# Fused attention and two expert layers on one core: the second half block's softmax in block 0 made on both groups at once and later

## The chip, the cores and the metric

One core of one Trainium2 chip. The metric is the device time of one execution in microseconds (us). The engines are TensorE (PE), VectorE (DVE), ScalarE (ACT), GpSimd (POOL) and the queue of the DMA issues (SP). Before the change three runs took 837.55 us in the median.

## What is computed

The reference is an attention over compressed keys and values, a gated layer, and a layer of eight experts of which each token takes two:

```python
a = softmax over the sequence of phi                      # 4 x 8 heads, 576 positions, 32 memory rows
k_m = einsum('bhsm,bhsd->bhmd', a, k)                     # 32 compressed keys a head
v_m = einsum('bhsm,bhsd->bhmd', a, v)
scores = (q @ k_m.T) / 8                                  # 576 x 32 a head
attn = exp(scores - max) / (sum(exp(scores - max)) + 1e-9)
x = attn @ v_m                                            # 2304 tokens of 512
g = x @ w_gate;  x = (silu(g) * (x @ w_val)) @ w_out      # 1536 wide
# then noisy top-2 gating over 8 experts, each relu(x @ w1) @ w2, summed with the gate's weights
```

Products that need float32's accuracy are made of three passes over tensors that are split in a high and a low part.

## The kernel before

**Blocks and slots.** The 2304 tokens are worked in eight half batches of 288 tokens, called blocks 0 to 7 (`BT = 288`, `NB = 8`). A block has twelve slots, one for each 128 columns of the gated layer (`NF1 = 12`). In a slot PE makes the gate and value products `pg` and `pv` (`gv`, L473, six products of 288 columns each) and the output products of two slots before (`down`, L502 in block 0, L506 later). ACT takes the tanh of `pg` (L481), DVE multiplies (`gate_act`, L486 and L487: "gate f" below is this step of slot f). L486 is also the last reader of the bank that the next slot's `pg` is written to. Block 0 differs from the others: its slots also unpack the packed weights w_a, in two halves, `top` on ACT (L204) and `low` on DVE (L208), and every second slot makes a projection of v_m with the gate and value weights (`proj_a` on PE, L346, with name pp; `proj_h` on ACT, L438, and `proj_b` on DVE, L443, its high and low parts, name pt).

**The softmax of a block.** It has two groups g of 128 rows (head parity), each a tile of 128 x 9 x 32. `s2_p` makes the scores on PE (psc), `s2_t` transposes them to SBUF on DVE (sm, L364), `s2_a` takes maxima and subtracts them (DVE, L370, L371), `s2_e` the exponential (ACT, L375), `s2_b` is `s2_sum` (sum, + 1e-9, reciprocal: L379 to L381) and `s2_norm` (scaling L386, transposition back L391), `s2_c` copies the result as the high part of X on ACT (L401), and `s2_d` subtracts it to get the low part on DVE (L404). X[i] holds both parts of both groups. In `gv` of a block i > 0 the first product reads group 0's high part and the second reads its low part.

**What sets the order.** All is written out by hand. `put(i, n, fn)` notes a step for a place n of block i, and `run(i, n)` carries out what is noted up to n; place 2f is the start of slot f, 2f + 1.5 lies behind its `gv`, and 2f + 1.99 is its end. The table `AT` has the places; the loop at L746 reads the list "s2" of block i - 1 for the softmax of block i, ten places: scores, transposition, maxima, exponential, then three for each group (`s2_b`, `s2_c`, `s2_d`). A pair of numbers splits a step: for maxima and exponential into group 0 and group 1. Each engine works its own instructions strictly in the order in which the program issues them. In block 0 the list makes the second half block's softmax X[1]: scores in slot 6, transpositions at 14, maxima at 17 and 17.9, exponentials at 17.1 and 19, group 0's sums at 19, group 1's at 21.1, the last subtraction at 23. "(1, 0)" below is slot 0 of block 1, where X[1] is first read.

The lines of `slot0` that set the order inside a slot of block 0:

```python
    gv(0, f)
    run(0, 2 * f + 1.5)
    ...
    gate_act(0, f)
    for k in todo:
        step(k)
    run(0, 2 * f + 1.99)
```

Of the kernel before, what the change touches and what calls it, by code (L numbers as in the profile page):

```python
# [7 lines left out]
F32 = mybir.dt.float32  # L8
# [12 lines left out]
B, H, S, D, M = 4, 8, 576, 64, 32  # L21
# [5 lines left out]
BT = S // 2  # L27
# [20 lines left out]
        2: (9, 9.92, 13.2, 13.9, 15, 17.9, 19, 19.9, 21, 21.9, 23, 23.9, 25, 25.9, 27),  # L48
    },
# [20 lines left out]
def r(ap):  # L70
    return ap.bitcast(F32R)
# [3 lines left out]
def moe_program(ctx, tc, xin, wa, wgn, nz, wb, out):  # L75
# [35 lines left out]
    gpool = right.enter_context(tc.tile_pool(name="gate", bufs=1, side="right"))  # L111
    att = left.enter_context(tc.tile_pool(name="att", bufs=1))
# [108 lines left out]
    for n in range(len(HOMES)):  # L221
# [26 lines left out]
    e_cap = const.tile([128, E], F32, name="e_cap")  # L248
    G.iota(e_cap, pattern=[[T, E]], base=CAPS, channel_multiplier=0,
           allow_small_or_imprecise_dtypes=True)  # L250
    kz = [const.tile([128, 2, 1 + n, D], F32, name=f"kz{n}") for n in range(2)]
    G.memset(kz[1], 0.0)
    TOP = [w1pool.tile([128, 2 * DM], FP16, tag="OS", name="top", bufs=4) for _ in range(4)]
    for t in TOP:
        G.memset(t, 0.0)
# [57 lines left out]

    def s1_cv(b, g, s=2, eng=None):
        st = ST[b, g][1]
        out = kz[g][:, :, g, :] if s == 2 else kz[g][:, s, g, :]
        p = TP.pop((b, g, s))
        if eng is None:
            V.tensor_scalar(out, p, st[:, 2:3], None, op0=OP.mult)
        else:  # L320
            A.activation(out, p, AF.Copy, scale=st[:, 2:3])

    def s1_d(b, g, s=2):

# [23 lines left out]
    def s2_p(i):  # L348
        p = [other([128, BT], "psc") for n in range(2)]
        by_heads(p, KM[i // 2][:, 0], QT[i])  # L350
        SM[i] = p

    def s2_first(g):

        p = {g: other([128, BT], "psc")}
        by_heads(p, KM[0][:, 0], QT[0], (g,))
        SM[0, g] = att.tile([128, BT // M, M], F32, tag="sm", name="sm", bufs=2)
        V.transpose(SM[0, g].rearrange("p a m -> p (a m)"), p[g])

    def s2_t(i):  # L360
        p = SM.pop(i)
        for n in range(2):
            SM[i, n] = att.tile([128, BT // M, M], F32, tag="sm", name="sm", bufs=2)
            V.transpose(SM[i, n].rearrange("p a m -> p (a m)"), p[n])  # L364

    def s2_a(i, g):
        na = BT // M
        sm = SM[i, g]
        rd = att.tile([128, 3, na], F32, tag="rd", name="rd", bufs=2)
        V.tensor_reduce(rd[:, 0, :], sm, axis=AX.X, op=OP.max)  # L370
        V.tensor_sub(sm, sm, rd[:, 0, :, None].to_broadcast([128, na, M]))  # L371
        SM[i, g] = (sm, rd)

    def s2_e(i, g):
        A.activation(SM[i, g][0], SM[i, g][0], AF.Exp, scale=1.0 / D ** 0.5)  # L375

    def s2_sum(i, g):
        sm, rd = SM[i, g]
        V.tensor_reduce(rd[:, 1, :], sm, axis=AX.X, op=OP.add)  # L379
        V.tensor_scalar(rd[:, 1, :], rd[:, 1, :], 1e-9, None, op0=OP.add)  # L380
        V.reciprocal(rd[:, 2, :], rd[:, 1, :])  # L381

    def s2_norm(i, g):
        na = BT // M
        sm, rd = SM[i, g]
        V.tensor_mul(sm, sm, rd[:, 2, :, None].to_broadcast([128, na, M]))  # L386
        if i or not g:
            at = att.tile([128, BT], F32, tag="at", name="at")
        else:
            at = gpool.tile([128, 2, 2, BT], F32, tag="x", name="ex")[:, 0, 0, :]  # L390
        V.transpose(at, sm.rearrange("p a m -> p (a m)"))  # L391
        SM[i, g] = at

    def s2_b(i, g):
        s2_sum(i, g)
# [350 lines left out]
    for i in range(1, NB):  # L746
        if i > 1:
            put(i - 1, 6, load_q, i)
        n = AT["s2"].get(i - 1, AT["s2"][2])
        put(i - 1, n[0], s2_p, i)  # L750
        put(i - 1, n[1], s2_t, i)
        for g in range(2):
            for m, fn in zip((n[2], n[3], *n[4 + 3 * g:7 + 3 * g]), (s2_a, s2_e, s2_b, s2_c, s2_d)):
                if fn is s2_b and isinstance(m, tuple):
                    put(i - 1, m[0], s2_sum, i, g)
                    put(i - 1, m[1], s2_norm, i, g)
                else:
                    put(i - 1, m[g] if isinstance(m, tuple) else m, fn, i, g)
# [802 lines left out]
```

## Time and profile before

| | us |
|---|---|
| median of 3 runs (lowest, highest) | 837.55 (836.06, 838.38) |
| the profiled execution | 840.57 |
| its span, first to last instruction | 838.8 |
| busy: PE, DVE, ACT, POOL | 824.1, 636.9, 391.6, 244.5 |
| mean granted clock of PE | 0.999 |

The profiled execution's time is a little above its span: what lies around the first and the last instruction is in the time and not in the span. Times in the rows below are counted from the span's start. A busy time alone does not tell what an engine costs; the chain of waits, followed back from the last instruction, does.

### The profile page before, as it was taken

How to read it: one execution, taken by the hardware profiler on the slowest of the kernel's cores; microseconds unless marked ns; L12 is line 12 of the kernel's file. 1: busy time of each engine (PE TensorE's matmuls, PEld its weight loads, DVE VectorE, ACT ScalarE, POOL GpSimd, SP SyncE). 2: the span in 40 equal slices, each digit the busy share in tenths (PEclk: the TensorE clock that was granted, in tenths of full speed). 3: DMA queues.
4: the chain of work that ended last, by engine and by line, in shares of the span. 5: the costliest groups of instructions: out<-in, count | busy, mean ns of one | idle time of the engine just before them, and what ended most of it. 6: DMA issues, size and time to landing. Idle time of an engine off the chain costs nothing.

```text
span 838.8 us, 16650 instructions
## 1 busy us (share of the span) xinstructions
PE 824.1 (98%) x6320; PEld 732.4 (87%) x6320; DVE 636.9 (76%) x1535; ACT 391.6 (47%) x804; POOL 244.5 (29%) x345
## 2 busy tenths in 40 slices
PE   8999999999999999999999999999999999999996
PEld 6777989999999998999999878988888888888885
DVE  5887688766867587868784597898889988899771
ACT  5765565333433334343444555446445454554430
POOL 2000012424243242553122223322415234145232
PEclk9999999999999999999999999999999999999999
DMA  9993649865327363449756983645574654654521
GB/s 345 402 399 122 199 161 326 256 221 151 106 74 219 86 209 85 132 115 234 212 173 174 231 234 73 137 134 119 121 168 104 158 127 99 164 139 111 161 85 64
DMA packets 79145, 143.20 MB, mean 171 GB/s; under 512 B 16176, under 2 KB 36880, under 8 KB 79056
## 3 DMA queue, kind: packets, MB, share of 16 engines
q1 hardware_dynamic: 59696, 100.66, 38.9%
q0 software_dynamic: 19360, 41.38, 20.8%
q8 instruction: 52, 0.85, 0.4%
q14 instruction: 37, 0.30, 0.1%
HBM read 105.34 MB, written 36.68 MB: 169 GB/s over the span
## 4 chain that ended last, share of the span: by engine, by line
PE 80%; DMA 8%; DVE 6%; issue 3%; ACT 1%; SPq 1%; POOL 1%; POOLq 0%; DVEq 0%; ACTq 0%
PE acc L1194 18%; PE ph L1178 17%; PE acc L506 16%; PE pg L473 10%; PE pv L473 9%; PE pp L346 3%; DMA xs<-R,gidx 2%; PE acc L502 2%; DMA wb<-wb 2%; DMA out<-pv,ix 1%; PE pT L528 1%; DMA early<-wa 1%; PE ph L987 1%; DMA kv<-xin 1%; PE pkv L310 1%
## 5 line engine op out<-in xcount | busy, mean ns | idle before, releaser
L1194 PE MATMUL acc<-ws,hs 128*128 128x512 f32 (+1 forms) x690 | 175.0, 394 | 0.0
L1178 PEld LDWEIGHTS ph<-xh,ws 128*128 128x128 f32 x1008 | 151.0, 188 | 9.7 <-ACT y L1217 0.7
L1178 PE MATMUL ph<-xh,ws 128*128 128x308 f32 x1008 | 157.4, 304 | 0.3 <-ACT y L1217 0.3
L1194 PEld LDWEIGHTS acc<-ws,hs 128*128 128x128 f32 (+1 forms) x690 | 122.7, 184 | 24.4
L506 PE MATMUL acc<-a,ro 128*128 128x288 f32 x576 | 116.4, 295 | 0.0
L1032 POOL DMA_INDIRECT out<-pv,ix x40 | 62.9, 1572 | 175.8 <-ACT pv L1024 65.5
L506 PE MATMUL acc<-a,os 128*128 128x288 f32 x432 | 106.0, 295 | 0.0
L473 PE MATMUL pg<-x,pt 128*128 128x288 f32 x576 | 101.3, 310 | 0.7 <-DVE pt L443 0.2
L473 PEld LDWEIGHTS pg<-x,pt 128*128 128x128 f32 x576 | 80.9, 188 | 18.5 <-issue 6.8
L506 PEld LDWEIGHTS acc<-a,ro 128*128 128x128 f32 x576 | 92.1, 188 | 0.0
L473 PE MATMUL pv<-x,pt 128*128 128x288 f32 x576 | 91.9, 295 | 0.0
L473 PEld LDWEIGHTS pv<-x,pt 128*128 128x128 f32 x576 | 81.7, 188 | 0.0
L670 POOL DMA_INDIRECT xs<-R,gidx x48 | 47.9, 999 | 115.9 <-DMA xs<-R,gidx 99.4
L486 DVE SCALAR_TENSOR_TENSOR ta<-ta,pg 128x288 f32<-128x288 f32 x84 | 37.7, 449 | 54.1 <-ACT ta L481 54.0
L506 PEld LDWEIGHTS acc<-a,os 128*128 128x128 f32 x432 | 74.1, 188 | 0.3 <-ACT ro L459 0.2
L481 ACT ACTIVATE ta<-pg 128x288 f32<-128x288 f32 x84 | 34.4, 409 | 80.9 <-PE pg L473 79.9
L463 POOL DMA_DIRECT2D os<-osl x72 | 40.8, 567 | 98.0 <-PE acc L506 57.9
L492 ACT ACTIVATE a<-ta 128x288 fp32r<-128x288 f32 x84 | 37.3, 444 | 68.5 <-DVE ta L487 66.7
L987 PE MATMUL ph<-xt,wm 128*128 128x384 f32 (+1 forms) x256 | 55.3, 306 | 0.0
L987 PEld LDWEIGHTS ph<-xt,wm 128*128 128x128 f32 x256 | 43.7, 189 | 2.6
L487 DVE TENSOR_TENSOR ta<-ta,pv 128x288 f32<-128x288 f32 x84 | 38.2, 454 | 8.7
L493 DVE TENSOR_TENSOR a<-ta,a 128x288 fp32r<-128x288 f32 x84 | 37.6, 448 | 5.8 <-ACT a L492 5.6
(241 smaller groups left out, 1453.0 us busy)
## 6 DMA issues: line engine op xcount, KB each, us to landing
wb<-wb SPq DMA_DIRECT2D x70, 512.0 KB
os<-osl POOLq DMA_DIRECT2D x72, 256.0 KB
kv<-xin SPq DMA_DIRECT2D x16, 576.0 KB
xl<-xs SPq DMA_DIRECT2D x40, 160.0 KB
stg<-wa SPq DMA_DIRECT2D x12, 511.8 KB
out<-zt SPq DMA_DIRECT2D x1, 5888.0 KB
xd<-R SPq DMA_DIRECT2D x8, 603.0 KB
qt<-xin SPq DMA_DIRECT2D x8, 576.0 KB
```

The costliest lines, as they stand in the source:

```text
L463: G.dma_start(r(lo), r(osl[f][:, :]))
L473: P.matmul(p, r(PT[f // 2, g][:, w, f % 2, 128 * a:128 * a + 128]), r(X[i][:, s, g, :]), start=(n == 0), stop=(n == 5))
L486: V.scalar_tensor_tensor(ta, ta, 1.0, pg, op0=OP.add, op1=OP.mult)
L487: V.tensor_mul(ta, ta, pv)
L492: A.activation(r(ah[:, 0, :]), ta, AF.Copy)
L493: V.tensor_sub(r(ah[:, 1, :]), ta, ah[:, 0, :])
L506: P.matmul(ACC[i][c], r(OS[i, f][w][:, o]), r(ah[:, s, :]), start=(f == 0 and n == 0), stop=(f == NF1 - 1 and n == 2))
L670: G.indirect_dma_start(out=xs[:, :], out_offset=bass.IndirectOffsetOnAxis(ap=RT[i][:, t, n:n + 1], axis=0), in_=R[i][:, t, :], in_offset=None)
L987: P.matmul(p, r(w[:, c]), r(x[:, k, b, :]), start=(m == 0), stop=(m == 11))
L1032: G.indirect_dma_start(out=out, out_offset=bass.IndirectOffsetOnAxis(ap=IX[e][:h, t:t + 1], axis=0), in_=PV[e, t][:h], in_offset=None, com ...
L1178: P.matmul(out, r(w[i][:, c + 128 * k:c + 128 * k + 128]), r(x[:, m, k, a]), start=(start and n == 0), stop=(n == 5), skip_group_check=not ...
L1194: P.matmul(AC2[e, t][:h, cols], r(HS[p][a][:, n, o]), r(w[b][:, n, cols]), start=(f == 0 and m == 0), stop=(f == NF2 - 1 and m == 2), skip ...
```

## The change

For block 0's list "s2" there are now seven places in the place of ten, which the loop takes as "both groups in one": maxima and subtraction at 21 (behind `gv` of slot 10), exponential at 21.02, sums to transposition at 21.9 (end of slot 10), copy at 22 (start of slot 11), subtraction at 23.55 (end of slot 11). To make that possible both groups lie in one tile (sm, rd and at), and each step takes a group number or 2 for both. Other blocks keep their places and still go group by group, in the new tiles. Three small things come with it: the first block's subtractions are one instruction, group 1's own tile `ex` is gone, and the two tiles kz with a padding of zeros become one without.

```diff
     "s2": {
-        0: (13.9, 14, (17, 17.9), (17.1, 19), 19, 19.9, 21, 21.1, 21.9, 23),
+        0: (13.9, 14, 21, 21.02, 21.9, 22, 23.55),
...
-    kz = [const.tile([128, 2, 1 + n, D], F32, name=f"kz{n}") for n in range(2)]
-    G.memset(kz[1], 0.0)
+    kz = const.tile([128, 2, 2, D], F32, name="kz")
...
-                P.transpose(p[:64 * g + 64, m, :], kz[g][:, m].rearrange("p n d -> p (n d)"), ident)
+                P.transpose(p[:64 * g + 64, m, :], kz[:, m, :g + 1].rearrange("p n d -> p (n d)"), ident)
...
+    na = BT // M
+
+    def groups(g):
+        return slice(0, 2) if g == 2 else slice(g, g + 1)
+
+    def flat(t, g):
+        return t[:, groups(g)].rearrange("p g a m -> p (g a m)")
+
+    def sm_tile(i):
+        SM[i, "s"] = att.tile([128, 2, na, M], F32, tag="sm", name="sm", bufs=1)
+        SM[i, "r"] = att.tile([128, 3, 2, na], F32, tag="rd", name="rd", bufs=1)
...
+    def s2_parts(i, g):
+        sm, rd = SM[i, "s"], SM[i, "r"]
+        sm = sm[:, groups(g)].rearrange("p g a m -> p (g a) m")
+        return sm, [rd[:, k, groups(g)].rearrange("p g a -> p (g a)") for k in range(3)]
+
     def s2_a(i, g):
-        na = BT // M
-        sm = SM[i, g]
-        rd = att.tile([128, 3, na], F32, tag="rd", name="rd", bufs=2)
-        V.tensor_reduce(rd[:, 0, :], sm, axis=AX.X, op=OP.max)
-        V.tensor_sub(sm, sm, rd[:, 0, :, None].to_broadcast([128, na, M]))
-        SM[i, g] = (sm, rd)
+        sm, rd = s2_parts(i, g)
+        V.tensor_reduce(rd[0], sm, axis=AX.X, op=OP.max)
+        V.tensor_sub(sm, sm, rd[0][:, :, None].to_broadcast(list(sm.shape)))
...
     def s2_norm(i, g):
-        na = BT // M
-        sm, rd = SM[i, g]
-        V.tensor_mul(sm, sm, rd[:, 2, :, None].to_broadcast([128, na, M]))
-        if i or not g:
-            at = att.tile([128, BT], F32, tag="at", name="at")
-        else:
-            at = gpool.tile([128, 2, 2, BT], F32, tag="x", name="ex")[:, 0, 0, :]
-        V.transpose(at, sm.rearrange("p a m -> p (a m)"))
-        SM[i, g] = at
+        sm, rd = s2_parts(i, g)
+        V.tensor_mul(sm, sm, rd[2][:, :, None].to_broadcast(list(sm.shape)))
+        if g != 1:
+            SM[i, "t"] = att.tile([128, 2, na, M], F32, tag="at", name="at")
+        V.transpose(flat(SM[i, "t"], g), flat(SM[i, "s"], g))
...
     def s2_d(i, g):
-        V.tensor_sub(r(X[i][:, 1, g, :]), SM.pop((i, g)), X[i][:, 0, g, :])
+        hi, lo = [X[i][:, k, groups(g)].rearrange("p g t -> p (g t)") for k in range(2)]
+        V.tensor_sub(r(lo), flat(SM[i, "t"], g), hi)
...
-        for g in range(2):
-            for m, fn in zip((n[2], n[3], *n[4 + 3 * g:7 + 3 * g]), (s2_a, s2_e, s2_b, s2_c, s2_d)):
+        for g in range(2) if len(n) > 7 else (2,):
+            k = 4 + 3 * (g % 2)
+            for m, fn in zip((n[2], n[3], *n[k:k + 3]), (s2_a, s2_e, s2_b, s2_c, s2_d)):
...
-    both(s2_d, 0)
+    s2_d(0, 2)
```

Lines behind L249 move by up to 13: L370 becomes L385, L371 L386, L379 L394, L391 L403, L401 L412, L404 L416, L473 L485, L481 L493, L486 L498, L502 L514.

DVE, before, from the projection split of slot 10 to gate 11 (a is the activation of a slot, pg and pv its gate and value products, ro and wa unpacked weights):

```order
L443 TENSOR_TENSOR pt<-pp,pt 128x512 x2
L208 SCALAR_TENSOR_TENSOR ro<-stx,top 128x512
L404 TENSOR_TENSOR x<-at,x 128x288
L379 TENSOR_REDUCE rd<-sm 128x9
L380 TENSOR_SCALAR rd<-rd 128x9
L381 RECIPROCAL rd<-rd 128x9
L386 TENSOR_TENSOR sm<-sm,rd 128x288
L391 STREAM_TRANSPOSE at<-sm 128x288
L486 SCALAR_TENSOR_TENSOR a_983<-a_983,pg 128x288
L487 TENSOR_TENSOR a_983<-a_983,pv 128x288
L208 SCALAR_TENSOR_TENSOR ro<-stx,top 128x512
L404 TENSOR_TENSOR x<-at,x 128x288
```

DVE, the change, from the same unpacking ro of slot 10 to the transposition; a_961 is slot 10's activation here (a_983 above):

```order
L208 SCALAR_TENSOR_TENSOR ro<-stx,top 128x512
L385 TENSOR_REDUCE rd<-sm 128x18
L386 TENSOR_TENSOR sm<-sm,rd 128x576
L498 SCALAR_TENSOR_TENSOR a_961<-a_961,pg 128x288
L499 TENSOR_TENSOR a_961<-a_961,pv 128x288
L208 SCALAR_TENSOR_TENSOR ro<-stx,top 128x512
L394 TENSOR_REDUCE rd<-sm 128x18
L395 TENSOR_SCALAR rd<-rd 128x18
L396 RECIPROCAL rd<-rd 128x18
L400 TENSOR_TENSOR sm<-sm,rd 128x576
L403 STREAM_TRANSPOSE at<-sm 128x576
```

Behind it DVE has gate 11, the last unpacking and `x<-at,x 128x576`. All of X[1]'s softmax on DVE now stands behind the unpacking of slot 10; before, group 0 and group 1's maxima stood in slots 8 and 9, and only group 1's sums stood here.

ACT in slots 10 and 11, before:

```order
L438 ACTIVATE pt<-pp 128x512 x2
L204 ACTIVATE top<-stx 128x512
L481 ACTIVATE a_983<-pg 128x288
L204 ACTIVATE top<-stx 128x512
L401 ACTIVATE x<-at 128x288
L481 ACTIVATE a_1016<-pg 128x288
L204 ACTIVATE top<-stx 128x512
```

ACT there, the change:

```order
L450 ACTIVATE pt<-pp 128x512 x2
L204 ACTIVATE top<-stx 128x512
L493 ACTIVATE a_961<-pg 128x288
L390 ACTIVATE sm<-sm 128x576
L204 ACTIVATE top<-stx 128x512
L412 ACTIVATE x<-at 128x576
L493 ACTIVATE a_997<-pg 128x288
L204 ACTIVATE top<-stx 128x512
```

The exponential of both groups stands between the tanh of slot 10 and an unpacking's first half, and the copy into x of both groups stands ahead of the tanh of slot 11; before, the exponentials stood in slots 8 and 9, and the copy there was group 1's alone.

PE's order is the same; what its instructions wait for differs at two places. At slot (1, 0) of the change, the first two gate products wait for DVE, the second for the low part of x:

```order
L485 MATMUL pg<-x,pt 128x288 [waits DVE_49] x2
L485 MATMUL pg<-x,pt 128x288 x4
L485 MATMUL pv<-x,pt 128x288 x6
```

Before, the first and the fourth of these waited, and the first of pv. The other place is the first product of the expert stage, which now waits for GpSimd also:

```order
L1000 MATMUL ph<-xt,wm 128x384 [waits DMAHW3_49,DVE_49,Pool_49]
```

## Rows read from the trace of the kernel before

**Rows 1.** The page, part 1: busy us (share of the span) and instructions.
```profile
PE 824.1 (98%) x6320; PEld 732.4 (87%) x6320; DVE 636.9 (76%) x1535; ACT 391.6 (47%) x804; POOL 244.5 (29%) x345
```

**Rows 2.** The chain of waits in block 0: start us, length us, what.
```profile
54.80 1.29 DVE pt L443 x2
...
63.12 0.49 DVE at L391
...
65.34 1.00 PE pg L473 x4
...
71.11 1.06 PE pg L473 x6
72.18 0.80 PE pv L473 x6
72.98 1.94 PE acc L502 x8
```

**Rows 3.** Timeline, slot 8 and the start of slot 9: start us, length us, instruction.
```profile
52.98 1.09 PE L346 MATMUL pp<-wa,km 64*32 64x256 f32 x32
...
55.84 1.18 PE L473 MATMUL pg<-x,pt 128*128 128x288 f32 x6
56.00 0.68 DVE L208 SCALAR_TENSOR_TENSOR wa<-stx,top 128x512 int32<-128x512 int32 x1
56.60 0.45 DVE L370 TENSOR_REDUCE rd<-sm 128x9 f32<-128x288 f32 x1
...
57.05 0.41 ACT L481 ACTIVATE a<-pg 128x288 f32<-128x288 f32 x1 [1.13 <-PE pg L473]
...
59.36 1.18 PE L473 MATMUL pg<-x,pt 128*128 128x288 f32 x6
```

**Rows 4.** Timeline, slots 9 to 11: in brackets the idle time before and its releaser.
```profile
60.58 0.41 ACT L481 ACTIVATE a<-pg 128x288 f32<-128x288 f32 x1 [0.62 <-PE pg L473]
...
61.26 1.23 PE L346 MATMUL pp<-wa,km 64*32 64x256 f32 x32
...
62.38 0.21 DVE L381 RECIPROCAL rd<-rd 128x9 f32<-128x9 f32 x1
...
63.63 0.44 ACT L401 ACTIVATE x<-at 128x288 fp32r<-128x288 f32 x1 [2.31 <-DVE at L391]
...
69.07 1.06 PE L473 MATMUL pg<-x,pt 128*128 128x288 f32 x6
...
70.61 0.45 DVE L486 SCALAR_TENSOR_TENSOR a<-a,pg 128x288 f32<-128x288 f32 x1
```

**Rows 5.** Groups of instructions from 54 to 80: count, busy us, mean ns.
```profile
L270 DVE TENSOR_REDUCE st<-phi 128x1 f32<-128x576 f32 x2 | 1.4, 746 | 0.0
...
L404 DVE TENSOR_TENSOR x<-at,x 128x288 fp32r<-128x288 f32 x2 | 0.9, 454 | 0.0
...
L453 DVE TENSOR_TENSOR os<-ro,os 128x512 fp32r<-128x512 f32 x1 | 0.7, 681 | 0.0
...
L452 ACT ACTIVATE os<-ro 128x512 fp32r<-128x512 f32 x1 | 0.6, 622 | 0.0
```

**Rows 6.** Stretches: length; busy PE, PEld, DVE, ACT, POOL; granted clock; DMA share; GB/s.
```profile
832.00:832.50 0.50, 0.05 (x1) 0.00 (x0) 0.41 (x2) 0.00 (x0) 0.00 (x0) 1.00 0.04 16
835.50:836.00 0.50, 0.00 (x0) 0.00 (x0) 0.00 (x0) 0.00 (x0) 0.00 (x0) 1.00 0.71 180
...
836.50:837.00 0.50, 0.00 (x0) 0.00 (x0) 0.00 (x0) 0.00 (x0) 0.00 (x0) 0.50 0.00 0
```

**Rows 7.** The same by two long stretches.
```profile
85.00:466.00 381.00, 381.00 (x3429) 349.79 (x3427) 271.17 (x859) 158.42 (x367) 119.84 (x230) 1.00 0.60 174
466.00:495.00 29.00, 26.61 (x160) 22.62 (x160) 21.88 (x43) 16.82 (x29) 7.28 (x5) 1.00 1.04 258
```

**Rows 8.** GpSimd's timeline (first row), and the chain of waits (second).
```profile
407.55 1.00 POOL L670 DMA_INDIRECT xs<-R,gidx  x1 [11.40 <-ACT wm L850]
...
402.80 2.10 PE ph L987 x12
```

More of the change, by code (lines that the diff above doesn't have):

```diff
@@ L315, in s1_cv @@
         st = ST[b, g][1]
-        out = kz[g][:, :, g, :] if s == 2 else kz[g][:, s, g, :]
+        out = kz[:, :, g, :] if s == 2 else kz[:, s, g, :]
         p = TP.pop((b, g, s))
@@ L356, in s2_first @@
         by_heads(p, KM[0][:, 0], QT[0], (g,))
-        SM[0, g] = att.tile([128, BT // M, M], F32, tag="sm", name="sm", bufs=2)
-        V.transpose(SM[0, g].rearrange("p a m -> p (a m)"), p[g])
+        if g == 0:
+            sm_tile(0)
+        V.transpose(flat(SM[0, "s"], g), p[g])
     def s2_t(i):
         p = SM.pop(i)
+        sm_tile(i)
         for n in range(2):
-            SM[i, n] = att.tile([128, BT // M, M], F32, tag="sm", name="sm", bufs=2)
-            V.transpose(SM[i, n].rearrange("p a m -> p (a m)"), p[n])
@@ L366, in s2_a @@
-    def s2_a(i, g):
-        na = BT // M
-        sm = SM[i, g]
-        rd = att.tile([128, 3, na], F32, tag="rd", name="rd", bufs=2)
-        V.tensor_reduce(rd[:, 0, :], sm, axis=AX.X, op=OP.max)
-        V.tensor_sub(sm, sm, rd[:, 0, :, None].to_broadcast([128, na, M]))
-        SM[i, g] = (sm, rd)
+            V.transpose(flat(SM[i, "s"], n), p[n])
+    def s2_parts(i, g):
+        sm, rd = SM[i, "s"], SM[i, "r"]
+        sm = sm[:, groups(g)].rearrange("p g a m -> p (g a) m")
+        return sm, [rd[:, k, groups(g)].rearrange("p g a -> p (g a)") for k in range(3)]
@@ L374, in s2_e @@
+    def s2_a(i, g):
+        sm, rd = s2_parts(i, g)
+        V.tensor_reduce(rd[0], sm, axis=AX.X, op=OP.max)
+        V.tensor_sub(sm, sm, rd[0][:, :, None].to_broadcast(list(sm.shape)))
     def s2_e(i, g):
-        A.activation(SM[i, g][0], SM[i, g][0], AF.Exp, scale=1.0 / D ** 0.5)
+        sm = flat(SM[i, "s"], g)
+        A.activation(sm, sm, AF.Exp, scale=1.0 / D ** 0.5)
     def s2_sum(i, g):
-        sm, rd = SM[i, g]
-        V.tensor_reduce(rd[:, 1, :], sm, axis=AX.X, op=OP.add)
-        V.tensor_scalar(rd[:, 1, :], rd[:, 1, :], 1e-9, None, op0=OP.add)
@@ L381, in s2_sum @@
-        V.reciprocal(rd[:, 2, :], rd[:, 1, :])
+        sm, rd = s2_parts(i, g)
+        V.tensor_reduce(rd[1], sm, axis=AX.X, op=OP.add)
+        V.tensor_scalar(rd[1], rd[1], 1e-9, None, op0=OP.add)
+        V.reciprocal(rd[2], rd[1])
     def s2_norm(i, g):
-        na = BT // M
-        sm, rd = SM[i, g]
-        V.tensor_mul(sm, sm, rd[:, 2, :, None].to_broadcast([128, na, M]))
-        if i or not g:
-            at = att.tile([128, BT], F32, tag="at", name="at")
-        else:
-            at = gpool.tile([128, 2, 2, BT], F32, tag="x", name="ex")[:, 0, 0, :]
@@ L391, in s2_norm @@
-        V.transpose(at, sm.rearrange("p a m -> p (a m)"))
-        SM[i, g] = at
+        sm, rd = s2_parts(i, g)
+        V.tensor_mul(sm, sm, rd[2][:, :, None].to_broadcast(list(sm.shape)))
+        if g != 1:
+            SM[i, "t"] = att.tile([128, 2, na, M], F32, tag="at", name="at")
+        V.transpose(flat(SM[i, "t"], g), flat(SM[i, "s"], g))
     def s2_b(i, g):
@@ L398, in s2_c @@
     def s2_c(i, g):
-        if g == 0:
+        if g != 1:
             X[i] = (gpool if i % 2 else att).tile([128, 2, 2, BT], F32, tag="x", name="x")
-        A.activation(r(X[i][:, 0, g, :]), SM[i, g], AF.Copy)
+        A.activation(r(X[i][:, 0, groups(g)].rearrange("p g t -> p (g t)")), flat(SM[i, "t"], g), AF.Copy)
     def s2_d(i, g):
-        V.tensor_sub(r(X[i][:, 1, g, :]), SM.pop((i, g)), X[i][:, 0, g, :])
+        hi, lo = [X[i][:, k, groups(g)].rearrange("p g t -> p (g t)") for k in range(2)]
+        V.tensor_sub(r(lo), flat(SM[i, "t"], g), hi)
     PT, OS, ACT1, ACC = {}, {}, {}, {}
```

## The prediction

> **What bounds the kernel now.** The page comes first: TensorE (PE) is busy for 98% of the span [rows 1]. So what counts is the time in which PE stands still, and the engine it then waits for. The chain of waits tells that for block 0, where the change lies [rows 2]. Before 54 us it is PE's; from 54.80 it runs over VectorE (DVE), with the softmax's transposition at 63.12 among its pieces, comes back to PE only at 65.34, and has PE waiting once more at 71.11, for the first gate products of block 1. From 71.11 on the pieces are PE's again, and between 85 and 466 PE is busy for 381.00 of 381 us [rows 7]: what block 0 loses or gains is neither given back nor grown there.
>
> Third view: the timeline of slot 8, the last projection slot without a stall of PE [rows 3]. It gives the pattern that slot 10 (also with a projection) would keep if nothing held it up. Counted from the start of the projection's products (52.98): DVE splits it at +1.82 [rows 2], the slot's gate products start at +2.86, DVE unpacks at +3.02 and is free for the next instruction at +3.62, ScalarE's (ACT's) tanh runs at +4.07, the next slot's gate products start at +6.38.
>
> Fourth view: the timeline of slots 9 to 11 [rows 4]. The projection of slot 10 starts at 61.26, so its gate products are due at 64.12 and those of slot 11 at 67.64. In fact the chain shows four of slot 10's held until 65.34, and slot 11's start at 69.07. The holder is DVE, which does softmax work ahead of gate 9, and with it ACT, whose split of the projection stands behind the softmax's copy at 63.63, which had waited 2.31 us for DVE.
>
> **What is removed.** From slots 8 and 9 DVE loses two maxima, two subtractions, one sum, one scaling, two small operations and one transposition: 6 x 0.45 + 2 x 0.21 + 0.49 = 3.6 us by the narrow rows [rows 2 to 4]. The unpackings then stand end to end, and gate 9 waits only for its tanh (60.58 + 0.41). So slot 11's gate products move from 69.07 to 67.64, a gain of **1.4 us** that lasts only if the next step can use it. PE's part of slot 11 is a gate half of 1.06 and a value half of 0.80 [rows 2, 4]; it would be done at 69.5.
>
> **What is put behind it.** All of X[1] is now made after the unpacking of slot 10, due at 61.26 + 3.02 = 64.28. Wide operations: a reduction of 576 columns stands in the trace with 746 ns; elementwise, 288 columns take 454 and 512 take 681 ns, 1.01 ns a column, which gives 746 for 576 too [rows 5]; the transposition 0.49 + 288 x 0.00101 = 0.78; ACT's copy, from 0.44 for 288 [rows 4] and 0.62 for 512 [rows 5], 0.67. Back to back the next one starts 0.03 behind the end; the small ones (0.21) stay. A handover between engines takes 0.04 to 0.05 (70.61 + 0.45 to 71.11) [rows 2, 4].
> - Maxima 64.88, subtraction 65.66, done at 66.41. Gate 10 follows on DVE (to 67.3; its tanh was over at 61.26 + 4.07 + 0.41 = 65.74).
> - Exponential on ACT 66.45 to 67.12; behind it in ACT's queue the first half of an unpacking (about 0.78, as long as the two halves beside it), to 67.83. The DVE half waits for it: 67.88.
> - Sum 68.48, small ones 69.26 and 69.47, scaling 69.71, transposition 70.49 to 71.27.
> - Copy on ACT from 71.31. The tanh of slot 11 stands behind it, though its input is there near 68.9, and runs from 71.9 to 72.30.
> - Gate 11 on DVE: 72.35 to 72.80, which frees the bank of the gate products; PE issues the first product of (1, 0) at 72.85. Second half of the gate 72.90, unpacking 73.27, subtraction that makes the low part of X[1] 73.87 to 74.62.
> - The second product of (1, 0) reads that low part: 74.67. Before it stood one sixth of 0.80 behind 71.11, at 71.24.
>
> **Sum:** 74.67 - 71.24 = **+3.4 us** for all that follows; the gain of 1.4 is contained in it. DVE is spared some 1.2 us in all (6 x 0.15 to 0.2 and two small operations), but what sets the end is the length of the path from 64.28, not that total.
>
> Bounds. If 576 columns cost only what 512 do (0.68 on DVE, 0.62 on ACT), six DVE operations lose 0.07 and two of ACT 0.05 each: +2.9. If they cost twice the narrow ones (0.90 and 0.88), it is 0.15 and 0.21 each: +4.7. I take 0.75, since a row has exactly this width. The start of the maxima rests on a pattern and may be off by 0.3 either way: 2.6 to 5.0 in all.
>
> Edits with no price: the zeroing of a padded tile on GpSimd goes, in the first us of the program, where nothing waits for GpSimd's next work for long; at the start of block 0 one subtraction of 0.75 replaces two of 0.45, but two products wait for its end where one did: 0, between -0.1 and +0.1. One wait is new far behind: PE's first expert product waits for GpSimd also. GpSimd stood idle for 11.40 us before 407.55, the product stands at 402.80 [rows 8], and the instruction at 407.55 is behind it in the program: 0.
>
> The profiled execution took 840.57 us (span 838.8), 3.0 above the median of the runs; I add the sum to that median: 837.55 + 3.4 = **841.0**. About 2.5 us (0.3%) is what a measurement of this kernel can tell from no change.
>
> [...] PE would stand from 69.5 to 72.85, give one product of 0.13, and stand again until 74.67. The longest stop in the trace is at its end: last product over at 832.05, granted clock still 1.00 in 835.50 to 836.00 and 0.50 in 836.50 to 837.00 [rows 6]. By these rows a stop of 3.4 us costs nothing in clock, and 5.2 with one product in it is open. [...]
>
> **Rivals.**
> - B: the clock falls to half in that stop. Then at least the rest of the step (5 x 0.13 + 0.80 = 1.45) takes twice as long, at most the output products of 1.94 behind it too [rows 2]: +1.5 to +3.4, middle 2.4, so 837.55 + 3.4 + 2.4 = 843.4. For it: the fall at the end. Against it: there it came after more than 3.9 us without any product.
> - C: the delay is absorbed later. PE is idle for 29.00 - 26.61 = 2.4 us between 466 and 495 [rows 7]. If the work it waits for there goes at its own pace, 3.4 - 2.4 = +1.0 is left: 838.6, no difference. Against it: that work starts from what PE's results release, so it should slide along.
> - D: not slower. X[1] is ready in time and the early gain is kept. The point from which this decides is 69.5, PE's own end of slot 11: if the low part of X[1] is written by then, (1, 0) starts there and not at 71.11, -1.6 us, 835.9; with a share of the saved 1.2 us of DVE, 835. It would need the path from 64.28 to take 5.2 us where I count 10.3, so the wide operations would have to cost next to nothing. The row of 746 ns speaks against it.
> - E: nothing changes, because the groups are still made one after the other. The order of the changed program has one instruction of 576 where two stood, which all but excludes it.
>
> **Chances.** Forecast 0.62, B 0.17, C 0.13, D 0.06, E 0.02. Of the forecast, 0.05 falls below +2.5 (low bound and a lucky measurement). Slower: 0.57 + 0.17 = 0.74. Faster: 0.04, of D. Same: 0.05 + 0.13 + 0.02 + 0.02 = 0.22. Range: the forecast's own bounds are 840.2 to 842.5; it is stretched down to 838.8 for a part of C and up to 844.2 for most of B; D, E, the rest of C and B's end, some 0.2, are left out.
>
> **What would show it.** Right: gate products of slot 11 near 67.6 instead of 69.07; PE idle for some 3 us before the first product of (1, 0) and near 2 us behind it, ended by DVE's subtraction into x; tanh of slot 11 directly behind the 576-wide copy; no softmax rows on DVE in slots 8 and 9, and gate 9 near 61.0. B would show as a granted clock under 1.00 near 73 to 78. Wrong: the second product of (1, 0) without a wait, or wide operations well under 0.65 us; and if that product waits as I say but the time grows by 1 us or less, PE's idle time between 466 and 495 must have shrunk.

## The result, and the profile after

| | before | after |
|---|---|---|
| median of five runs (lowest, highest), us | 836.89 (836.06, 838.38) | 844.81 (843.7, 846.57) |
| ratio to before, 95% interval | | 1.0093 [1.0075, 1.011] |
| the profiled execution, its span, us | 840.57, 838.8 | 843.7, 841.9 |
| mean granted clock of PE in the profiled execution | 0.999 | 0.994 |

Slower by 7.9 us where +3.4 was forecast, and outside the range that was given. Two of the twelve runs of one kernel below (every wide step in a place of its own) took 1142.63 and 1336.53 us; they count as slow, for a cause that no trace shows, and its ratio leaves them out. The page's busy times, which answer to [rows 1], show next to nothing of it:

```profile
PE 825.0 (98%) x6320; PEld 736.0 (87%) x6320; DVE 636.3 (76%) x1526; ACT 391.5 (47%) x802; POOL 244.7 (29%) x344
```

PE is busy for 0.9 us longer than before, though no product was added, and DVE for 0.6 less. The place is block 0's end. Its timeline answers to [rows 4] (start us, length us, instruction; in brackets the idle time before and what ended it):

```profile
61.36 0.45 DVE L498 SCALAR_TENSOR_TENSOR a<-a,pg 128x288 f32<-128x288 f32 x1
...
64.46 1.18 PE L485 MATMUL pg<-x,pt 128*128 128x288 f32 x6
64.62 0.68 DVE L208 SCALAR_TENSOR_TENSOR ro<-stx,top 128x512 int32<-128x512 int32 x1
65.22 0.75 DVE L385 TENSOR_REDUCE rd<-sm 128x18 f32<-128x576 f32 x1
...
66.80 0.68 ACT L390 ACTIVATE sm<-sm 128x576 f32<-128x576 f32 x1 [0.71 <-DVE sm L386]
...
68.00 1.17 PE L485 MATMUL pg<-x,pt 128*128 128x288 f32 x6
68.19 0.69 DVE L208 SCALAR_TENSOR_TENSOR ro<-stx,top 128x512 int32<-128x512 int32 x1 [0.51 <-ACT top L204]
...
70.88 0.78 DVE L403 STREAM_TRANSPOSE at<-sm 128x576 f32<-128x576 f32 x1
71.69 0.68 ACT L412 ACTIVATE x<-at 128x576 fp32r<-128x576 f32 x1 [3.54 <-DVE at L403]
72.28 0.39 ACT L493 ACTIVATE a<-pg 128x288 f32<-128x288 f32 x1
...
72.70 0.45 DVE L498 SCALAR_TENSOR_TENSOR a<-a,pg 128x288 f32<-128x288 f32 x1 [1.05 <-ACT a L493]
...
73.21 0.40 PE L485 MATMUL pg<-x,pt 128*128 128x288 f32 x1 [3.25 <-DVE a L498]
...
74.24 0.75 DVE L416 TENSOR_TENSOR x<-at,x 128x576 fp32r<-128x576 f32 x1
...
75.04 1.57 PE L485 MATMUL pg<-x,pt 128*128 128x288 f32 x5 [1.43 <-DVE x L416]
```

In the kernel before gate 9 stands here:

```profile
63.52 0.42 DVE L486 SCALAR_TENSOR_TENSOR a<-a,pg 128x288 f32<-128x288 f32 x1
```

Gate 9 is on time (61.36, against 63.52 before), so are the products of slots 10 and 11 (64.46 and 68.00): the gain of the removed work came. Then the path from the unpacking at 64.62 runs as the prediction drew it, and PE stands for 3.25 us before the first product of (1, 0) and for 1.43 before the second. The wide steps cost what was taken for them, which answers to [rows 5] (groups from 54 to 80; count, busy us, mean ns):

```profile
L403 DVE STREAM_TRANSPOSE at<-sm 128x576 f32<-128x576 f32 x1 | 0.8, 778 | 0.0
L386 DVE TENSOR_TENSOR sm<-sm,rd 128x576 f32<-128x576 f32 x1 | 0.8, 759 | 0.0
...
L394 DVE TENSOR_REDUCE rd<-sm 128x18 f32<-128x576 f32 x1 | 0.7, 745 | 0.0
```

```profile
L412 ACT ACTIVATE x<-at 128x576 fp32r<-128x576 f32 x1 | 0.7, 683 | 3.5 <-DVE at L403 3.5
```

The stretches answer to [rows 6, 7] (length; busy PE, PEld, DVE, ACT, POOL; granted clock; DMA share; GB/s):

```profile
72.00:74.00 2.00, 0.40 (x1) 0.19 (x1) 1.19 (x3) 1.33 (x3) 0.00 (x0) 1.00 0.00 0
74.00:76.00 2.00, 0.96 (x4) 0.96 (x5) 2.00 (x4) 0.00 (x0) 0.00 (x0) 0.56 0.00 0
76.00:78.00 2.00, 2.00 (x10) 2.00 (x10) 0.77 (x2) 1.35 (x4) 0.00 (x0) 0.50 0.03 8
78.00:80.00 2.00, 2.00 (x6) 1.43 (x5) 1.35 (x6) 1.01 (x3) 0.00 (x0) 0.50 0.00 0
80.00:82.00 2.00, 2.00 (x11) 1.52 (x10) 0.00 (x0) 0.00 (x0) 0.00 (x0) 0.73 0.00 0
82.00:84.00 2.00, 2.00 (x26) 1.84 (x28) 0.45 (x1) 1.69 (x4) 0.00 (x0) 1.00 0.00 0
85.00:466.00 381.00, 380.53 (x3438) 349.47 (x3431) 273.19 (x863) 161.21 (x374) 118.10 (x229) 1.00 0.59 176
466.00:495.00 29.00, 29.00 (x173) 26.12 (x172) 20.77 (x42) 15.82 (x26) 9.00 (x6) 1.00 1.06 256
```

Before, the clock was 1.00 between 85 and 495, as it was in every slot's stretch from 19 to 72. After, it falls within 74 to 76, stays at half until it comes back within 80 to 82, and PE is busy all that time from 75.04 on: the same products at half speed. The first product of (1, 0), at 73.21, still ran at 1.00. Quarter-us stretches put the fall at 74.3 and the return at 81.1, 6.8 us.

**A measure for what follows.** The runs of one kernel differ by some us, so the sum is followed in the traces: the *lag* of a run at a slot is the start of that slot's value products less the start of the same products in the kernel before's trace. A positive lag is later. The lag at slot 9 of block 0 is not the change's and is taken off: it lies between -0.80 and 1.62 us in the traces, and the 1.62 belongs to a kernel with the instructions of the kernel before (the one with 32 bytes added, below). For the change it stands at 0.34 in slot 9, -0.97 in slot 11, 6.63 in the second slot of block 1, 7.44 at the start of block 7, 7.92 at its end: 6.3 us are lost at the passage from block 0 to block 1, 0.8 between there and block 7, 0.5 in block 7's slot 8, 7.6 in all.

### The profile page after: what moved, and what is told of

Its sections match the earlier page's. It is cut to its first block, busy times and chain, and to the rows that moved or that the text cites. A ratio compares the mean times of both kernels' runs of the same rounds, so it can differ in the third digit from the quotient of the medians.

```text
span 841.9 us, 16638 instructions
## 1 busy us (share of the span) xinstructions
PE 825.0 (98%) x6320; PEld 736.0 (87%) x6320; DVE 636.3 (76%) x1526; ACT 391.5 (47%) x802; POOL 244.7 (29%) x344
## 4 chain that ended last, share of the span: by engine, by line
PE 90%; DVE 4%; DMA 3%; issue 1%; ACT 1%; SPq 1%; POOL 0%; POOLq 0%; DVEq 0%; ACTq 0%
PE acc L1207 18%; PE ph L1191 17%; PE acc L518 15%; PE pg L485 9%; PE pv L485 8%; PE ph L1000 7%; PE acc L1018 7%; PE pp L345 3%; PE acc L514 3%; DMA out<-pv,ix 1%; DMA stg<-wa 1%; PE pT L540 1%; PE pkv L309 1%; PE plg L551 1%; PE psc L345 1%
## 5 line engine op out<-in xcount | busy, mean ns | idle before, releaser
L485 PE MATMUL pg<-x,pt 128*128 128x288 f32 x576 | 102.0, 312 | 5.6 <-DVE a L498 3.3
L485 PEld LDWEIGHTS pg<-x,pt 128*128 128x128 f32 x576 | 81.6, 189 | 22.3 <-issue 6.2
L485 PE MATMUL pv<-x,pt 128*128 128x288 f32 x576 | 93.0, 297 | 0.0
L485 PEld LDWEIGHTS pv<-x,pt 128*128 128x128 f32 x576 | 82.7, 189 | 0.0
L498 DVE SCALAR_TENSOR_TENSOR ta<-ta,pg 128x288 f32<-128x288 f32 x84 | 37.7, 448 | 58.8 <-ACT ta L493 58.7
L493 ACT ACTIVATE ta<-pg 128x288 f32<-128x288 f32 x84 | 34.3, 409 | 85.2 <-PE pg L485 85.1
```

The costliest lines, as they stand in the source:

```text
L485: P.matmul(p, r(PT[f // 2, g][:, w, f % 2, 128 * a:128 * a + 128]), r(X[i][:, s, g, :]), start=(n == 0), stop=(n == 5))
L498: V.scalar_tensor_tensor(ta, ta, 1.0, pg, op0=OP.add, op1=OP.mult)
```

## The experiments

**The new tiles alone**, with the old list of ten places:

```diff
-        0: (13.9, 14, 21, 21.02, 21.9, 22, 23.55),
+        0: (13.9, 14, (17, 17.9), (17.1, 19), 19, 19.9, 21, 21.1, 21.9, 23),
```

> The change with block 0's old list of ten places: both groups in one tile, one kz without padding, one subtraction at the start, but the softmax of the second half block group by group where it stood before. Theory 1 (the late places cost a stop of PE of 3.4 us, and the clock that falls in it 3 more): as before, within 0.3%, ratio 0.998 to 1.003, the granted clock at 1.00 from 70 to 85, and block 1's second value products near 76.2. Theory 2 (the new tiles cost part of the 7.9 us, since everything was already 0.3 us late at 31 us and drifted by 0.8 more between blocks 1 and 7): +1 us or more, with both the early lag and the drift in its trace.

Measured: 838.98 us (836.56 to 842.1, 12 runs), before 836.88, ratio 1.0017 [1.0001, 1.0033]. The lag grows by 0.75 us from block 1 to block 7, and only in blocks 2, 4 and 6; the change's grows by 0.81 in the same places. So a part of the loss has nothing to do with the new places in time: the growth of theory 2 is there, its early lag is not (0.14 in slot 9). The lag also rises by 0.40 in slot 10; that is not the tiles' doing, for it rises there by 0.34 in one of the runs below whose instructions are those of the kernel before (64 bytes added), and by nothing in another with the new tiles. The two rises make 1.1 us; the median is 2.1 higher, and the rest is not explained.

**The change, with the clock held.** Small products that nobody reads fill PE's stop ahead of (1, 0):

```diff
+    def keep_warm(n):
+        for _ in range(2):
+            p = other([128, 128], "warm")
+            for _ in range(n):
+                P.matmul(p, ones, ones, start=True, stop=True)
+
+    put(0, 23.2, keep_warm, 39)
```

> The change, with 78 small products of ones by ones put on PE between the value products of slot 11 and the first gate products of block 1, where PE has nothing to do; they feed nothing. Theory 1: they end near 74.9, the granted clock stays 1.00, the second gate product still waits for DVE until about 75, and block 1's second value products come 3.4 to 3.8 us later than before instead of 6.3 to 6.6; the time is 3 us below that of the change, ratio to before 1.005 to 1.006. Rival (the low clock is a consequence and not a cause of the lost time, or PE's time after the stop is lost to something else such as DVE or ACT being behind): the time stays at that of the change, ratio 1.009.

Measured: 844.1 us (841.35 to 846.59, 6 runs), ratio 1.0085 [1.0064, 1.0105]. PE's timeline and two stretches of its trace:

```profile
70.01 4.53 PE L841 MATMUL warm<-ones 128*128 128x128 bf16 x78
74.34 0.38 PE L485 MATMUL pg<-x,pt 128*128 128x288 f32 x1
75.24 0.93 PE L485 MATMUL pg<-x,pt 128*128 128x288 f32 x5 [0.52 <-DVE x L416]
```

```profile
74.00:76.00 2.00, 1.48 (x16) 1.27 (x14) 2.00 (x4) 0.00 (x0) 0.00 (x0) 1.00 0.00 0
76.00:78.00 2.00, 2.00 (x13) 1.75 (x12) 1.64 (x5) 1.80 (x5) 0.00 (x0) 1.00 0.00 0
```

The second product still waits for DVE's low part, so the added work costs nothing there; the clock stays at 1.00, and the lag in block 1 is 3.99 - 0.54 = 3.45 us where the change has 6.63 - 0.34 = 6.29. By the traces the half clock cost 2.84 us, and what is left is the forecast's sum. The medians do not show this: 844.1 lies too near the change's 844.81, the intervals overlap, and a ratio of 1.0085 is nearer to the rival's; only the lowest runs (841.35 and 843.7) differ by about as much, and the trace is that of the lowest. What the other runs lost is not shown, so the same products are used once more in another form below.

**The wide steps in the early places:**

```diff
-        0: (13.9, 14, 21, 21.02, 21.9, 22, 23.55),
+        0: (13.9, 14, 17, 17.1, 19, 19.9, 21),
```

> The change with other places for the same wide steps: maxima and subtraction at 17, exponential at 17.1, sums to transposition at 19, copy at 19.9, subtraction at 21, which is where group 0's steps stood before. Theory 1 (not the width but the late places cost time): low part of X[1] ready near 67.5, the first gate products of block 1 no longer wait for it, and since DVE has 1.2 us less to do than before ahead of gate 11 they start 0.5 to 1.3 us earlier than the 71.11 of before; ratio 0.998 to 1.000. Rival (wide steps are bad wherever they stand, because each holds DVE's queue for 2.8 us at a time while gate 9 and the projection's split wait): first gate products of block 1 at 71.5 or later, ratio 1.001 or more.

Measured: 839.21 us (837.13 to 842.56, 12 runs), ratio 1.0027 [1.0015, 1.004]. That is its rival's answer. There is no long stop (the longest wait of PE in its timeline is the 1.09 us ahead of 66.48) and no fall of the clock at this passage (the first six products of block 1 take 1.06 us, as in the kernel before), yet the lag rises from 0.90 us in slot 9 to 1.62 in block 1. Its timeline:

```profile
57.49 0.75 DVE L385 TENSOR_REDUCE rd<-sm 128x18 f32<-128x576 f32 x1
...
61.58 0.38 ACT L493 ACTIVATE a<-pg 128x288 f32<-128x288 f32 x1
...
65.15 0.41 DVE L498 SCALAR_TENSOR_TENSOR a<-a,pg 128x288 f32<-128x288 f32 x1
65.26 0.68 ACT L412 ACTIVATE x<-at 128x576 fp32r<-128x576 f32 x1 [3.30 <-DVE at L403]
...
66.48 0.53 PE L485 MATMUL pg<-x,pt 128*128 128x288 f32 x2 [1.09 <-ACT pt L450]
```

The tanh of slot 9 was over at 61.96, but gate 9 runs at 65.15, behind the 576-wide sum, scaling and transposition; ACT's copy waits for the transposition, and the split of the projection stands behind the copy. The stall of the kernel before at this place is made longer: a wide step holds whatever is queued behind it until both groups are done.

**The copy behind the tanh of slot 11:**

```diff
-        0: (13.9, 14, 21, 21.02, 21.9, 22, 23.55),
+        0: (13.9, 14, 21, 21.02, 21.9, 23, 23.55),
```

> The change with the copy of the high part at 23 instead of 22, so behind the tanh of slot 11 in ACT's queue. Theory 1 prices the tanh's wait behind the copy: gate 11 starts when DVE's transposition ends, near 71.7 instead of 72.7, and the first gate product of block 1 near 72.2 instead of 73.2; the low part of x is ready some 0.5 us earlier, near 74.5. The clock falls all the same, so 0.5 us is gained, ratio to before 1.008 to 1.009. Rival (the place of the copy sets the end): 1 us or more gained.

Measured: 843.08 us (842.04 to 843.22, 4 runs), ratio 1.0067 [1.0048, 1.0086]; lag in block 1 5.82 - 0.75 = 5.07, which is 1.2 better than the change.

```profile
72.83 0.61 PE L485 MATMUL pg<-x,pt 128*128 128x288 f32 x1 [2.46 <-ACT x L412]
...
74.88 1.57 PE L485 MATMUL pg<-x,pt 128*128 128x288 f32 x5 [1.45 <-DVE x L416]
```

```profile
72.00:74.00 2.00, 0.61 (x1) 0.29 (x1) 1.38 (x4) 1.35 (x2) 0.00 (x0) 0.69 0.00 0
...
78.00:80.00 2.00, 2.00 (x6) 1.38 (x6) 1.28 (x6) 0.85 (x3) 0.00 (x0) 0.60 0.00 0
```

With the start of the program taken off, the second product comes 0.6 us earlier than in the change (74.88 - 0.75 against 75.04 - 0.34). The rest of the 1.2 is the clock: by quarter-us stretches it falls at 72.8 and is back at 79.6, 6.8 us again, but PE's steady work begins at 74.88, so 4.7 us of it are done at half speed where the change does 6.0. The 0.6 is the copy's, as its theory had it; the clock's part is not the copy's doing, for a second trace of the change itself, below, has a lag of 4.88.

**The place of X in memory.** The new tiles move X of the even blocks from byte 130208 of a partition to 130816; X of the odd blocks stays, and most other tiles move by 512 bytes or more. Two runs: the new tiles with the old list and 32 bytes more in rd, and the kernel before with nothing but an unused tile of 32 bytes.

```diff
-        SM[i, "r"] = att.tile([128, 3, 2, na], F32, tag="rd", name="rd", bufs=1)
+        SM[i, "r"] = att.tile([128, 62], F32, tag="rd", name="rd", bufs=1)[:, :6 * na].rearrange(
+            "p (k g a) -> p k g a", k=3, g=2)
```

> The new tiles with the old list of ten places, as in the run of the tiles alone, but the small tile rd ahead of X made 32 bytes larger, so that X of the even blocks begins at byte 130848 of a partition and not at 130816. In the kernel before it begins at 130208, in the odd blocks at 173920; these and 130848 leave 32 when divided by 64, 130816 leaves 0. In the run of the tiles alone the products fell behind the kernel before by 0.28 us in block 2, 0.38 in block 4 and 0.1 to 0.15 in block 6, about 0.03 us a slot, and by nothing in the odd blocks. Theory (where X of the even blocks lies slows its readers): the lag stands still from block 1 to block 7, within 0.1 us, and the time is 0.8 us under that of the run of the tiles alone, near 838.2. Rival 1 (any of the other moves in memory, by 512 bytes or in the other tiles): the lag grows by 0.8 us again. Rival 2 (the joint tile for both groups makes a wait in each even block): the same growth, and PE would show idle time there.

```diff
         rd = att.tile([128, 3, na], F32, tag="rd", name="rd", bufs=2)
+        if (i, g) == (0, 1):
+            att.tile([128, 8], F32, tag="pad", name="pad")
```

> The kernel before with one thing added, an unused tile of 32 bytes ahead of X of the even blocks, which then begins at byte 130240 of a partition instead of 130208 and leaves 0 when divided by 64, as in the change. No instruction is added, taken away or moved. Theory (where X lies): the products fall behind those of the kernel before by 0.3 to 0.4 us in each of the blocks 2, 4 and 6 and by nothing in the odd ones, 0.8 us in all: 837.7, ratio 1.001. Rival (it is another consequence of the new tiles): no lag grows, 836.9, ratio 1.000. The times alone can hardly tell these apart, the lag by block can.

Measured: 837.39 us (835.72 to 837.97, 11 runs), ratio 1.000 [0.9988, 1.0013], for the first; 837.65 (836.64 to 840.82, 12 runs), 1.0008 [0.9992, 1.0024], for the second, before 836.84. Two more runs with 64 bytes in place of 32, of one execution each, were to tell whether whole multiples of 64 are what counts:

> As the run with the pad in the new tiles, but 64 bytes of pad and not 32: X of the even blocks begins at byte 130880, which leaves 0 when divided by 64, as 130816 of the change does. Theory (what counts is whether X begins at a whole multiple of 64 bytes): the lag grows in blocks 2, 4 and 6 by about 0.8 us in all, as with 130816. Rival (130816 was a bad place for another reason, such as where it lies against other tiles): the lag grows by 0.3 us or less, as with 130848.

> The kernel before with an unused tile of 64 bytes ahead of X of the even blocks: it begins at byte 130272, which leaves 32 when divided by 64, as 130208 of the kernel before does. Theory (whole multiples of 64 bytes): no lag grows, within 0.1 us from block 1 to block 7. Rival (any move of X costs something, or the place against other tiles counts): the lag grows by 0.3 us or more, as it did by 0.66 with 130240.

Measured: 836.71 and 838.00 us, before 836.93; single times tell nothing here. The growth is read off two rows of each trace, the first value products of slot 1 of block 1 and of slot 0 of block 7. The kernel before, and the kernel before with 32 bytes:

```profile
76.21 0.96 PE L473 MATMUL pv<-x,pt 128*128 128x288 f32 x6
...
360.66 0.96 PE L473 MATMUL pv<-x,pt 128*128 128x288 f32 x6
```

```profile
77.85 0.96 PE L475 MATMUL pv<-x,pt 128*128 128x288 f32 x6
...
362.95 0.96 PE L475 MATMUL pv<-x,pt 128*128 128x288 f32 x6
```

284.45 us lie between the first two and 285.10 between the others.

| X of the even blocks at byte | tiles | from row to row, us | growth, us |
|---|---|---|---|
| 130208 | old (the kernel before) | 284.45 | 0 |
| 130240 | old, 32 bytes added | 285.10 | 0.65 |
| 130272 | old, 64 bytes added | 285.01 | 0.56 |
| 130816 | new | 285.20 | 0.75 |
| 130848 | new, 32 bytes added | 284.64 | 0.19 |
| 130880 | new, 64 bytes added | 284.83 | 0.38 |

The second row differs from the first in nothing but X's address, so that this alone costs 0.65 us over three blocks is shown. The row of 130816 is the run of the tiles alone; the five other traces at that address have 0.73 to 0.97, and the three others at 130848 have 0.16 to 0.20, so these are not draws of one execution. The larger rd takes away 0.56 of the new tiles' 0.75. The rule of 64 is not borne out: 130272 should have cost nothing and costs 0.56, which is its rival's answer, and 130880 falls between its two answers. Why one address is better than another stays open.

**Both by-products taken out**: the change, with the small products and with rd 32 bytes larger.

> The change with both suspected by-products taken out at once: 78 small products ahead of the first product of block 1, as in the run that held the clock, and rd larger by 32 bytes. Theory (three separate costs: path +3.4, clock +2.8, place of X +0.8): only the path is left, lag of 3.4 to 3.6 us from the second slot of block 1 to the end of block 7 once the lag at slot 9 is taken off, no growth in the even blocks: 840.3, ratio 1.004. Rival 1 (the clock's share is not removed but put off): granted clock under 1.00 somewhere in block 1 or 2 and a lag of over 5 us behind it. Rival 2 (the growth in the even blocks comes from something else in the change): lag near 4.3 at the end, 841.1.

Measured: 841.91 us (839.6 to 844.05, 8 runs), ratio 1.0055 [1.0038, 1.0073]. The lag in block 1 is 3.17 + 0.29 = 3.46 us, at the start of block 7 3.33 + 0.29 = 3.62, and the clock does not fall later either (0.998 in the mean of this execution, 0.994 in the change's). That is the path alone. At the end of block 7 the lag is 4.11, near the second rival's 4.3, but not for its reason: the even blocks take 0.16 of it, and 0.49 come at once in slot 8 of block 7, as in the change. The median is 5.1 us above that of the kernel before and 2.4 below that of the change on the same chip (844.31, below). Where the last 1 us of the median comes from is not shown, but in this trace PE stands idle for 0.96 us behind the blocks, where the change has no such idle time:

```profile
466.00:495.00 29.00, 28.04 (x166) 24.12 (x165) 19.90 (x38) 15.70 (x26) 8.87 (x6) 1.00 1.03 261
```

**Every wide step in a place of its own**, with the larger rd:

```diff
+                if fn is s2_a and g == 2 and isinstance(m, tuple):
+                    put(i - 1, m[0], s2_max, i, g)
+                    put(i - 1, m[1], s2_sub, i, g)
...
-        0: (13.9, 14, 21, 21.02, 21.9, 22, 23.55),
+        0: (13.9, 14, (15, 17), 17.1, (19, 21), 21.05, 21.95),
```

> The change's tiles (rd larger by 32 bytes as in the run with the pad) and the wide steps, with each of them in a place of its own: maxima in slot 7 ahead of its gate, where VectorE stood idle for 0.64 us, subtraction in slot 8 ahead of its gate, exponential behind the tanh of slot 8, sums in slot 9 ahead of its gate, scaling and transposition in slot 10 ahead of its gate, the copy behind the tanh of slot 10, the low part behind that gate. Theory (what the change loses is the length of one chain of seven wide steps put behind the unpacking of slot 10; the widening itself saves VectorE time): gate 9 some 1.4 us earlier than in the kernel before, the projection of slot 10 split without a wait for the copy, gate products of slot 11 1.3 to 1.4 us earlier, first product of block 1 1.0 to 1.5 us earlier than the 71.11 of the kernel before and no second stop behind it, clock at 1.00: 835.4 to 835.9, ratio 0.998 to 0.999. Rival 1 (the maxima of 0.75 us do not fit the idle 0.64 and hold the split of slot 8 by 0.1 us or more, and the sums hold gate 9): gain 0.5 us or less. Rival 2 (wide steps are slower wherever they stand, as in the run of the early places, +0.7): slower by 0.3 to 0.7 us.

Measured: 836.18 us in the median of all twelve runs, lowest 834.57; by ten of them ratio 0.9983 [0.9969, 0.9997].

```profile
52.46 0.74 DVE L386 TENSOR_REDUCE rd<-sm 128x18 f32<-128x576 f32 x1
...
61.92 0.40 DVE L506 SCALAR_TENSOR_TENSOR a<-a,pg 128x288 f32<-128x288 f32 x1
...
62.13 1.08 ACT L458 ACTIVATE pt<-pp 128x512 fp32r<-128x512 f32 x2 [1.46 <-PE pp L345]
...
67.33 1.17 PE L493 MATMUL pg<-x,pt 128*128 128x288 f32 x6
...
69.49 1.06 PE L493 MATMUL pg<-x,pt 128*128 128x288 f32 x6 [0.20 <-DVE a L506]
```

Gate 9 is at 61.92, the split waits for nothing of the softmax, slot 11's products come at 67.33, and the first product of (1, 0) at 69.49, with no second stop. The lag goes from -0.32 to -1.63: 1.3 us gained at the passage to block 1. By the last slot of block 7 it is -0.87, so 0.55 of the gain is left: 0.2 goes in the even blocks, 0.35 in slot 8 of block 7, 0.2 in its slot 11. Since that is hardly more than the runs differ by, the kernel was run once more beside the change itself:

> The run with every wide step in its own place once more, on the same chip as the change itself, since its gain of 1.1 us in the lag and of 0.7 us in the medians is about as large as the spread of the runs. Theory (PE's stalls in slots 9 to 11 are gone for good): lag against the kernel before of -1.2 to -1.4 us from block 1 on once the lag of slot 9 is taken off, 835.4 to 836.4, ratio 0.997 to 0.9995. Rival (the first result was the draw of the runs): a ratio of 1.000 or more, though the lag is the same, which would mean that the expert stage takes the gain back.

> The change itself once more, unaltered, for more runs beside the same runs of the kernel before: the earlier comparison had five. Theory (path 3.4, clock 2.8, place of X and the like 0.8): lag of 7.0 to 7.2 us at the end of block 7 once the lag of slot 9 is taken off, lowest run some 7 us above the lowest of the kernel before, 843.9 to 844.8 in the median, the granted clock at half for 6.5 to 7 us from near 74 us. Rival (the clock's fall is a matter of the single execution): executions near 841 among the runs, those whose clock stayed up.

Measured: 835.93 us (835.3 to 837.67, 11 runs), ratio 0.999 [0.9981, 0.9999]. The lag goes from 0.69 to -0.60 in block 1 and stands at 0.12 in the last slot of block 7: 1.3 us gained and 0.58 kept, as in the first trace. So it is 0.1% faster than the kernel before, in an interval whose upper end is 0.9999, and 1% faster than the change. The change: 844.31 us (842.95 to 844.7, 5 runs), ratio 1.0087 [1.0073, 1.0101]. Its new trace has a surprise:

```profile
74.00:76.00 2.00, 0.57 (x2) 0.39 (x2) 2.00 (x4) 0.00 (x0) 0.00 (x0) 0.85 0.00 0
76.00:78.00 2.00, 2.00 (x10) 2.00 (x10) 1.22 (x3) 0.78 (x2) 0.00 (x0) 0.50 0.03 8
78.00:80.00 2.00, 2.00 (x9) 1.69 (x9) 1.39 (x7) 1.58 (x5) 0.00 (x0) 0.80 0.00 0
```

The stops of PE are the same (3.24 and 1.43 us), but the clock falls later, at 75.4, and is back at 78.8: 3.4 us at half speed, and the lag in block 1 is 5.80 - 0.92 = 4.88. So that execution lost only 1.4 us to the clock where the first lost 2.84. The clock fell in both traces; how long it stays down differs from one execution to the next, and the expectation of 6.5 to 7 us was wrong. No run came near 841, so the rival's runs in which the clock stays up were not seen.

## Why the prediction was wrong, point by point

- **The bound, the place and the direction** were right: PE at 98%, DVE's softmax behind slot 10 as the new holder, slower.
- **The gain of 1.4 us at slot 11** came: its products start at 68.00, which is 67.66 without the 0.34 us by which the whole program is late; 67.64 was forecast.
- **The path from 64.28** was right step by step: transposition 70.54 (70.49 forecast), copy 71.35 (71.31), first product 72.87 (72.85), second 74.70 (74.67), each with 0.34 taken off. Two of the times forecast on ACT (67.83 and 71.9) stand some 0.08 us before the end of the instruction ahead, which the working does not say; the trace bears it out (copy 71.69 and 0.68 long, tanh at 72.28). The tanh of slot 11 does stand directly behind the copy, and the wide steps (745 to 778 ns on DVE, 683 on ACT) cost what the row of exactly that width had given. The sum of +3.4 was measured alone as 3.45 and 3.46.
- **The step that failed is the one that put the clock's term at nothing.** The prediction read from the program's end that "a stop of 3.4 us costs nothing in clock", left 5.2 us with one product in it open, added up the path alone, and gave rival B, the clock at half in that stop, 0.17. The runs showed 2.84 us for the clock in the change's first trace and 1.43 in its second, and with the stop filled by small products a clock of 1.00 and the path alone. The rows of the end [rows 6] were one stop in one execution: there the clock was still 1.00 more than 3.9 us after the last product. In the two traces of the change it fell 4.3 and 4.8 us after the last product of slot 11, with one product of 0.40 in between; in the run with the late copy it fell 2.4 us after, ahead of any product. In the change's first trace the group behind the second stop ran at 0.50 (76 to 78), the one product directly behind the stop of 3.25 us at 1.00.
- **B's price** was +1.5 to +3.4, middle 2.4; measured were 2.84, inside, and 1.43, just under. B's time of 843.4 is 1.4 below the median of the change, and it has neither of the two terms that follow.
- **"Edits with no price"** failed in one item that was not on the list: the new tiles move X of the even blocks, and that costs about 0.6 to 0.8 us over blocks 2, 4 and 6. Another 0.5, in block 7, was not on it either. The other edits cost nothing that the traces show; the expert stage's first product, which waits for GpSimd too, starts at 410.72 against 402.80 [rows 8], 7.92 later, which is the lag that it inherits.
- **Rival C** (absorbed between 466 and 495): PE has no idle time there after (29.00 of 29.00), but the profiled execution of before had 2.4 us there and took 3.7 us more than the median of its runs. Such idle time belongs to that execution: the two kernels with the same instructions, 64 and 32 bytes added, have 0.00 and 0.36 us there. So there was nothing to absorb the delay in, and adding the sum to the median and not to that execution's own time was right.

```profile
466.00:495.00 29.00, 29.00 (x182) 25.94 (x181) 21.41 (x44) 16.73 (x29) 7.84 (x6) 1.00 1.04 252
466.00:495.00 29.00, 28.64 (x177) 25.29 (x176) 22.31 (x45) 17.71 (x31) 7.60 (x5) 1.00 1.02 251
```

- **Left open**: 0.5 us in slot 8 of block 7, which every run with the list of seven places has (0.33 to 0.5) and none with ten. In all eight traces with seven places DVE stands idle for 0.46 us in slot 6 ahead of the second half of the gate, and in none of the others; what holds it is not shown. Open too is why X's address matters, and what the part behind the blocks adds to a single run.

The whole: 3.45 (path) + 2.84 (clock) + 0.8 (tiles, in the even blocks) + 0.5 (block 7) = 7.6 us in the first execution, and 6.2 by the lag at the end of block 7 in the second; between the medians of the two comparisons lie 7.9 and 7.2.

## What to carry to other kernels

A stop of the bounding engine can have a second price, its clock (2.84 and 1.43 us here), and one stop that went unpunished in a trace does not show that the next will. When a stop of some us appears, add the cost of the following products at half rate (0.50 here) to the forecast as a term of its own; small products that filled the stop kept the clock up in two traces here (1.00 from 74 to 78 in one, 0.998 in the mean of the whole execution in the other). Merging two steps into one wide step saves DVE time (0.15 us a pair here) but holds whatever is queued behind it for 0.75 us at a time and not 0.45, so give every wide step its own gap, not one place for all. An edit that only resizes a tile moves others: compare the addresses of what the inner loop reads. And follow a small gain to the end: of the 1.3 us of the last kernel less than half was left behind block 7.

## What was not expected of the hardware

- The fall of the clock keeps no fixed distance from the last product: 2.4 us in one run, 4.3 and 4.8 in two executions of one kernel. The time at half speed was 3.4 us in one execution of the change, 6.8 in the other. And the same instructions can fare differently: in the kernel before with 32 bytes added the granted clock was 0.50 from 10.5 to 17.25 us, in the kernel before 1.00 (in the mean of the whole executions 0.993 and 0.999).
- A tile's address: the kernel before with X moved by 32 bytes, and not an instruction changed, loses 0.27 us in each of blocks 2 and 4, some 0.02 us a slot. No run here shows whether what PE loses (0.65 us over three blocks at 130240, nothing at 130208) is a wait for another engine.
